# An FFT stage hidden in a matmul pipeline: folds and first-stage groups at other steps

## The chip, the cores and the metric

One core of a Trainium2 chip runs the whole program. The metric is the device time of one execution in microseconds; lower is better. The page of the profile names the engines PE (TensorE, matmuls), PEld (its weight loads), DVE (VectorE), ACT (ScalarE), POOL (GpSimd) and SP (SyncE, which here only issues DMAs).

## The reference

Two parts follow each other. The first is the real part of a two-dimensional FFT over sequence and model dimension of each of 8 batches; the second is a feed-forward block with a quick GELU on all 8 x 3008 tokens.

```python
X = np.fft.fft(x, axis=1)          # x: (8, 3008, 256) float32
X = np.fft.fft(X, axis=2)
x = X.real.astype(np.float32).reshape(8 * 3008, 256)
h = x @ w_in                       # (256, 2048)
g = h * (1.0 / (1.0 + np.exp(-1.702 * h)))
return (g @ w_out).astype(np.float32)   # w_out: (2048, 256)
```

## The kernel before

The FFT over the sequence is done in two stages of small matrix products (3008 = 47 x 64); the FFT over the model dimension is folded into `w_in`. The feed-forward block takes the result as its input. It is one long pipeline of **steps**: `steps` lists (batch, block, half, p) for 8 batches, 3 blocks, 2 halves and p = 0 to 7, so 384 steps `t`, 48 per batch. `t0 = 48 b` is the first step of batch b, and p = t mod 8. A run of 8 steps with one block and one half is one output tile of up to 256 tokens (226 in the second half of block 0, where `width(t)` is smaller); the 8 steps go over the hidden dimension in pairs.

In a step t (from step 8 on) the loop at the end of the kernel issues: `begin(t, 1)`, matmuls into a PSUM bank x (`halves`, L184); `forward(t)`, a GELU by ACT (L597); `product(t - 3)`, the second product of an earlier step (L184, tile o); `small_products` (L678, tile low), products of a fast matrix multiplication whose operands DVE makes; `begin(t + 1)`; `backward(t)` on DVE (L604), which reads the PSUM bank x; `doubled` (L600) and `activate_back` (L607) on ACT; `sums(t, gpsimd)` on POOL (L615, L616), which waits for L607; `sums(t - 1, vector)` on DVE in even steps (L622, L623), which needs the POOL sums; `deeper` on DVE (L644), which makes operands of `small_products`. Once every 8 steps an output tile is finished: ACT copies it (L747, L749, issued at p = 2), DVE adds (L750, L751, L779, worked at p = 3 and 4, then L761 and L797), ACT swaps halves at p = 4 (L787 to L789), DVE transposes (L730, issued at p = 5 and 6), and SP stores.

Beside this pipeline lies the FFT of the **next** batch, hung on steps by `at(t, fn, ...)`; what hangs on a step is issued at its end, in the order of the `at` calls, and each engine works its queue in order.

- `load_x(b + 2, k)`, four pieces, at t0 + 31, 33, 35, 37 (5 later for b = 0), SP: loads x into the only buffer `xt`, each after `paced`, a DMA of one element that waits for a result of that step and so holds SP's queue back.
- `fold1(b + 1, c, part)`, 16 **folds** per batch (c = 0 to 7, part 0 and 1), POOL, in place in `xt`. Part 0 is L225 and L227, part 1 is L230 and L231; the first one also makes the tile e (L218 to L220).
- `mix1(b + 1, m)`, four first-stage **groups** per batch, PE (L255) into two PSUM banks, then ACT copies back into `xt` (`mixed`, L263): one copy at once, the other in the next step behind `forward`. Group m needs folds 4m to 4m + 3 (counted as 2c + part). Its banks are the one that step t's x had, so it waits for `backward(t)`, and b2. Group 0 has 22 matmul instructions (8 of them on e), the others 16.
- `spill(b + 1, half, m)`, two DMAs per group, SP, one step after the group; later `fill` reads the result back.
- `stage2(b, blk)` at t0 + 8, 24 and 40 for the next block: PE matmuls L365 and DVE transposes L372.

A step with `mix1` or `stage2` is `special`, the one behind it is `after`: the ACT copies of `middle` (L585) for the step two ahead are then made one step later, and more of `product` is put ahead of `begin(t + 1)`.

Before the change the folds of a batch b >= 1 lay one a step at t0 + 6 to t0 + 21, and the groups at t0 + 12, 15, 19 and 23 (p = 4, 7, 3, 7). In batch 0 they lay at 11 to 26, and at 16, 20, 25 and 28. Batch 7 has none, since no batch follows.

Of the kernel before, what the change touches and what calls it, by code (L numbers as in the profile page):

```python
# [112 lines left out]
def kernel(ctx: ExitStack, tc, x, w_in, w_out, tab1, tab2, out):  # L113
    nc = tc.nc
# [807 lines left out]
    finish_out(0)  # L922

    extra, early = {}, {}

    def at(t, fn, *args):
        extra.setdefault(t, []).append((fn, args))
# [23 lines left out]
    for b in range(B):  # L951
        t0 = b * NBLK * NF
        late = 0 if b else 5
        if b + 2 < B:
            for k in range(3):
                at(t0 + 11 + k, paced, t0 + 11 + k)
                at(t0 + 11 + k, turn, b + 2, k)
        if b + 1 < B:
            for c in range(NCH):
                for part in range(2):  # L960
                    at(t0 + 6 + 2 * c + part + late, fold1, b + 1, c, part, nc.gpsimd)
                if c % 2:
                    k = t0 + 9 + 2 * c + late + (c == (5 if late else 1))
                    at(k, mix1, b + 1, c // 2)
                    for half in range(2):
                        at(k + 1, spill, b + 1, half, c // 2)
            for blk in range(NBLK):
                at(t0 + 27 + blk + late, paced, t0 + 27 + blk + late)
                at(t0 + 27 + blk + late, fill, b + 1, 4 * blk, 4 * blk + 4)
            if b + 2 < B:  # L970
                for k in range(4):
                    at(t0 + 31 + 2 * k + late, paced, t0 + 31 + 2 * k + late)
                    at(t0 + 31 + 2 * k + late, load_x, b + 2, k)
            at(t0 + 36 + 3 * (late > 0), rotate, b + 1)
        for blk in range(NBLK):
            nxt = (b, blk + 1) if blk + 1 < NBLK else (b + 1, 0)
            if nxt[0] < B:
                at(t0 + blk * NF + 8, stage2, *nxt)
                at(t0 + blk * NF + 9, nyquist_out, *nxt)
                at(t0 + blk * NF + 10, nyquist, *nxt)  # L980
# [123 lines left out]
```

## Time and profile before

| What | Value |
|---|---|
| Runs before | 1854.57, 1856.98, 1858.54 us; median 1856.98 us |
| The profiled execution | 1857.67 us; its span 1855.9 us; granted clock 0.999 |
| PE, PEld, DVE, ACT, POOL busy | 1838.7, 1401.5, 1514.7, 1151.2, 971.2 us |
| Folds: mean of L225, L227, L230, L231 | 0.47, 1.50, 0.89, 1.06 us, 56 of each |
| POOL sums L615, L616 | 0.94 and 0.94 us on average, 376 of each |

Busy time within a step differs much between values of p. Eight steps of batch 2 in which no fold and no group lies, from the busy times in windows of the trace (the window of p = 4 also holds `rotate`):

| p | window, us | length | DVE busy | ACT busy | POOL busy |
|---|---|---|---|---|---|
| 0 | 647.99:652.76 | 4.77 | 2.99 | 2.96 | 2.38 |
| 1 | 652.76:657.09 | 4.33 | 2.27 | 2.15 | 1.15 |
| 2 | 657.09:661.86 | 4.77 | 2.99 | 2.96 | 2.38 |
| 3 | 661.86:666.19 | 4.33 | 3.34 | 2.27 | 0.90 |
| 4 | 666.19:671.05 | 4.86 | 4.79 | 4.53 | 1.87 |
| 5 | 671.05:675.41 | 4.36 | 4.26 | 2.15 | 1.93 |
| 6 | 675.41:680.18 | 4.77 | 4.63 | 3.71 | 2.64 |
| 7 | 680.18:684.51 | 4.33 | 4.04 | 2.41 | 2.13 |

How to read it: PE has work almost all the time, so the length of a step is the time from one step's first matmul to the next step's; the first matmul of step t is the L184 row with tile x that follows the products of step t - 1. A step without extras takes 4.77 us at even p and 4.33 us at odd p (less in the narrower tile). What a group costs is read from how much longer its step and the ones behind it are than the same steps of batch 7. A POOL operation hung on step t is worked at the beginning of step t + 1, since POOL's sums of step t come first and wait for the end of step t.

### The profile page before, as it was taken

To read this page: it belongs to the slowest core of one execution; us is meant where nothing else is said; L and a number is where in the kernel's file an instruction comes from. 1 tells how busy PE (TensorE), PEld (TensorE's weight loads), DVE (VectorE), ACT (ScalarE), POOL (GpSimd) and SP (SyncE) were. 2 spreads that over 40 slices of the span, in tenths; PEclk is the share of its full clock that TensorE was granted. 3 is DMA by queue.
4 is the path that set the end of the run, shared out by engine and by line. 5 is a ranking of instruction groups with operands and counts; after the bars stand their busy time and mean duration, and the time that the engine had idled before them with its cause. 6 is when DMAs were issued, how large, how long until landed. Compare 5 with 4: busy or idle time off the path is not lost.

```text
span 1855.9 us, 56072 instructions
## 1 busy us (share of the span) xinstructions
PE 1838.7 (99%) x23722; PEld 1401.5 (76%) x23722; DVE 1514.7 (82%) x2112; ACT 1151.2 (62%) x2241; POOL 971.2 (52%) x1053
## 2 busy tenths in 40 slices
PE   8999999999999999999999999999999999999998
PEld 4677777777777777777777777777777777778776
DVE  6988778888788877987789878888888888878874
ACT  5756666666666656666566666666666666656663
POOL 4776446744367434773348633476445754434442
PEclk9999999999999999999999999999999999999999
DMA  8821340215012340223302132121411111100111
GB/s 265 196 61 34 84 68 19 72 49 102 19 38 53 73 84 13 51 50 88 59 13 64 45 86 53 18 75 35 103 30 24 36 46 36 30 19 13 23 20 24
DMA packets 149706, 105.31 MB, mean 57 GB/s; under 512 B 106057, under 2 KB 130665, under 8 KB 148896
## 3 DMA queue, kind: packets, MB, share of 16 engines
q1 hardware_dynamic: 146624, 99.68, 23.7%
q8 instruction: 187, 3.06, 0.7%
q10 hardware_dynamic: 2832, 2.05, 0.5%
q14 instruction: 63, 0.52, 0.1%
HBM read 64.41 MB, written 48.05 MB: 61 GB/s over the span
## 4 chain that ended last, share of the span: by engine, by line
PE 90%; DVE 5%; ACT 3%; DMA 1%; issue 1%; DVEq 0%; ACTq 0%
PE x L184 33%; PE o L184 26%; PE low L678 23%; PE o L678 4%; PE ps L255 2%; DVE big L644 2%; PE ps L365 1%; DVE big L779 1%; PE psw L184 1%; DMA xt<-in_x_dram 1%; DVE big L604 1%; ACT x L585 1%; DVE big L622 0%; DMA small<-in_tab_dram 0%; ACT g L597 0%
## 5 line engine op out<-in xcount | busy, mean ns | idle before, releaser
L615 POOL TENSOR_TENSOR big<-big 128x256 f32<-128x256 f32 (+1 forms) x376 | 352.0, 936 | 828.7 <-ACT big L607 676.9
L184 PE MATMUL x<-pq,wcs 128*64 128x256 f32 (+1 forms) x6016 | 769.0, 376 | 1.9 <-ACT g L597 1.6
L644 DVE TENSOR_TENSOR big<-big 128x512 f32<-128x512 f32 (+1 forms) x736 | 618.9, 855 | 23.1 <-PE low L678 4.7
L184 PE MATMUL o<-big,wo 128*64 128x256 f32 (+1 forms) x4800 | 620.8, 375 | 0.1
L184 PEld LDWEIGHTS x<-pq,wcs 128*64 128x64 f32 x6016 | 412.2, 137 | 186.1 <-issue 15.0
L184 PEld LDWEIGHTS o<-big,wo 128*64 128x64 f32 x4800 | 341.8, 137 | 147.8 <-DVE big L622 0.5
L597 ACT ACTIVATE g<-x 128x512 f32<-128x512 f32 (+1 forms) x376 | 221.7, 590 | 369.9 <-PE x L184 368.6
L604 DVE TENSOR_TENSOR big<-g,x 128x512 f32<-128x512 f32 (+1 forms) x376 | 249.9, 665 | 212.8 <-ACT big L600 212.6
L585 ACT ACTIVATE x<-nb,af 128x256 f32<-128x256 f32 (+1 forms) x752 | 352.9, 469 | 76.2 <-DVE pq L372 63.1
L678 PE MATMUL low<-big 128*64 128x128 f32 (+1 forms) x5888 | 382.9, 270 | 0.0
L678 PEld LDWEIGHTS low<-big 128*64 128x64 f32 x5888 | 337.6, 137 | 29.2
L616 POOL TENSOR_TENSOR big<-big 128x256 f32<-128x256 f32 (+1 forms) x376 | 351.5, 935 | 0.0
L600 ACT ACTIVATE big<-x 128x512 f32<-128x512 f32 (+1 forms) x376 | 219.2, 583 | 128.2 <-PE x L184 122.5
L607 ACT ACTIVATE big<-big 128x512 f32<-128x512 f32 (+1 forms) x376 | 231.9, 617 | 46.6 <-DVE big L604 44.4
L678 PE MATMUL low<-big,wo 128*64 128x128 f32 (+1 forms) x2944 | 220.5, 271 | 0.2
L678 PEld LDWEIGHTS low<-big,wo 128*64 128x64 f32 x2944 | 171.3, 137 | 4.5 <-DVE big L644 1.6
L623 DVE TENSOR_TENSOR big<-big 128x512 f32<-128x512 f32 (+1 forms) x188 | 166.6, 886 | 6.5
L622 DVE TENSOR_TENSOR big<-big 128x512 f32<-128x512 f32 (+1 forms) x188 | 137.1, 729 | 6.1 <-POOL big L615 6.1
L779 DVE TENSOR_TENSOR big<-big,low 128x512 f32<-128x512 f32 (+3 forms) x184 | 109.0, 609 | 3.5
L678 PEld LDWEIGHTS o<-big,wo 128*64 128x64 f32 x1472 | 92.3, 137 | 24.9
L678 PE MATMUL o<-big,wo 128*64 128x128 f32 (+1 forms) x1472 | 110.1, 270 | 0.0
L227 POOL TENSOR_TENSOR xt<-xt 111x510 f32<-111x510 f32 x56 | 83.7, 1495 | 4.4
(95 smaller groups left out, 964.5 us busy)
## 6 DMA issues: line engine op xcount, KB each, us to landing
out_dram<-os SPq DMA_DIRECT2D x284, 64.0 KB
t<-Td SPq DMA_DIRECT2D x22, 512.0 KB
Td<-xt SPq DMA_DIRECT2D x56, 192.0 KB
xt<-in_x_dram SPq DMA_DIRECT2D x14, 512.0 KB
xt<-Xr SPq DMA_DIRECT2D x14, 512.0 KB
nb<-Nd SPq DMA_DIRECT2D x23, 256.0 KB
out_dram<-os SPq DMA_DIRECT2D x96, 56.0 KB
Xr<-in_x_dram SPq DMA_DIRECT2D x7, 752.0 KB
```

What stands on the lines that cost most here:

```text
L184: nc.tensor.matmul(out[c0:c0 + 64], lhsT=lhs[:, c0:c0 + 64], rhs=rhs, skip_group_check=True, **how)
L585: nc.scalar.activation(x[:, i * 256:i * 256 + n], nbt[b, blk][:, hh * 256:hh * 256 + n], ACTF.Copy, scale=af1[:, f:f + 1])
L597: nc.scalar.activation(two(g[:], n), two(xb[t][:], n), ACTF.Copy, scale=2.0)
L600: nc.scalar.activation(front(t), two(xb[t][:], width(t)), ACTF.Gelu_apprx_sigmoid)
L604: nc.vector.tensor_tensor(back(t), two(gt.pop(t)[:], n), two(xb.pop(t)[:], n), op=ALU.subtract)
L607: nc.scalar.activation(back(t), back(t), ACTF.Gelu_apprx_sigmoid)
L615: eng.tensor_tensor(right(t, S1, n), left(t, A21, n), right(t, A22, n), op=ALU.add)
L616: eng.tensor_tensor(left(t, S3, n), left(t, A11, n), left(t, A21, n), op=ALU.subtract)
L622: eng.tensor_tensor(s2, s1, a11, op=ALU.subtract)
L623: eng.tensor_tensor(s4, a12, s2, op=ALU.subtract)
L644: nc.vector.tensor_tensor(out, i0, i1, op=how)
L678: nc.tensor.matmul(o, lhsT=lhs, rhs=rhs, start=first_in, stop=(p == NP - 2), skip_group_check=True)
```

## The change

From batch 1 on, folds and groups no longer follow a formula but a table. The list of folds and the list of groups give steps relative to t0, the third row for all batches from b = 2 on, so that negative numbers lie in the batch before. The table's first row repeats what batch 0 had. The spills stay one step behind their groups. `load_x`, `fill`, `rotate` and `stage2` stay where they are.

```diff
+    PLANS = ((range(11, 27), (16, 20, 25, 28)), ((-1, 0, 1, 1, 2, 7, 7, 9, 10, 15, 15, 16, 16, 17, 17, 18), (7, 15, 19, 23)),
+             ((-9, -7, -7, -6, -1, 0, 1, 1, 2, 7, 9, 10, 15, 16, 17, 17), (-1, 7, 15, 23)))
...
         if b + 1 < B:
+            folds, groups = PLANS[min(b, 2)]
             for c in range(NCH):
                 for part in range(2):
-                    at(t0 + 6 + 2 * c + part + late, fold1, b + 1, c, part, nc.gpsimd)
+                    at(t0 + folds[2 * c + part], fold1, b + 1, c, part, nc.gpsimd)
                 if c % 2:
-                    k = t0 + 9 + 2 * c + late + (c == (5 if late else 1))
+                    k = t0 + groups[c // 2]
                     at(k, mix1, b + 1, c // 2)
                     for half in range(2):
                         at(k + 1, spill, b + 1, half, c // 2)
```

In values of p: groups go from 4, 7, 3, 7 to 7, 7, 3, 7 in batch 1 and to 7, 7, 7, 7 in batches 2 to 6. Folds go from every p to p = 7, 0, 1 and 2, with two folds hung on one step in some places (in batch 1 at t0 + 1, 7, 15, 16 and 17; from batch 2 on at t0 - 7, 1 and 17), and none at the steps with `stage2`.

## The prediction, made before the changed kernel ran

> **What bounds the kernel.** I read the page first, busy times and the chain that ended last:
>
> ```profile
> PE 1838.7 (99%) x23722; PEld 1401.5 (76%) x23722; DVE 1514.7 (82%) x2112; ACT 1151.2 (62%) x2241; POOL 971.2 (52%) x1053
> ...
> PE 90%; DVE 5%; ACT 3%; DMA 1%; issue 1%; DVEq 0%; ACTq 0%
> ```
>
> PE is the bound, and its matmuls stay. So the change can only win the time in which PE is held up, and that is on the chain as DVE and ACT. How much there is: busy times in two windows, 16 steps from t0 + 8 on, in batch 2 (four groups, 16 folds) and in batch 7 (none). Columns: window, its length, then busy time (and count) of PE, PEld, DVE, ACT, POOL, clock, DMA.
>
> ```profile
> 533.93:610.20 76.27, 75.68 (x1032) 58.37 (x1029) 67.71 (x88) 47.47 (x96) 59.07 (x67) 1.00 0.22 55
> 1658.43:1728.69 70.26, 70.22 (x963) 55.99 (x961) 57.26 (x87) 44.47 (x90) 29.36 (x34) 1.00 0.10 20
> ```
>
> The FFT of the next batch costs 6.01 us here. DVE's busy time is 10.45 us higher with one instruction more: its instructions are held while POOL folds.
>
> **What a group costs at each place.** PE's timeline of batch 2 (start, length, engine, line, what, count). First t0 + 12 (p = 4, group 0), then t0 + 15 (p = 7, group 1), then t0 + 20, the step behind group 2 at t0 + 19 (p = 3):
>
> ```profile
> 552.62 0.93 PE L184 MATMUL x<-pq,wcs 128*64 128x226 f32 x8
> ...
> 556.07 0.94 PE L678 MATMUL low<-big 128*64 128x113 f32 x16
> 557.37 0.32 PE L255 MATMUL ps<-e,w 47*64 47x129 f32 x1 [0.35 <-DVE big L604]
> ...
> 558.83 0.98 PE L184 MATMUL x<-pq,wcs 128*64 128x226 f32 x8
> ```
> ```profile
> 570.64 0.55 PE L184 MATMUL o<-big,wo 128*64 128x226 f32 x4
> 571.12 1.09 PE L255 MATMUL ps<-xt,w 47*64 47x256 f32 x16
> 572.15 1.08 PE L184 MATMUL x<-pq,wcs 128*64 128x256 f32 x8
> ```
> ```profile
> 590.37 1.08 PE L184 MATMUL x<-pq,wcs 128*64 128x256 f32 x8
> ...
> 594.32 1.04 PE L678 MATMUL low<-big 128*64 128x128 f32 x16
> 595.59 1.08 PE L184 MATMUL x<-pq,wcs 128*64 128x256 f32 x8 [0.23 <-ACT g L597]
> ```
>
> At **p = 7** nothing waits. Group 1 takes 572.15 - 571.12 = 1.03 us, 0.10 more is lost going into it (570.64 to 571.12 is 0.48 for rows that take 0.38 elsewhere) and 0.05 in the first row behind it: 1.18 us, and the same at t0 + 23.
>
> At **p = 4** step t0 + 12 lasts 558.83 - 552.62 = 6.21 us; in batch 7 it lasts 1681.19 - 1676.97 = 4.22 us. So 1.99 us, and 0.15 in the next step (3.99 us against 3.83), 0.05 in the one after: 2.19. The chain of waits from 549.5 to 557.3 is DVE alone (L644, L750, L751, L604, four L779, three L644, L604): group 0 waits for L604 to leave the bank, and L604 stands behind the tile's additions, which fall on p = 3 and 4, in a step where DVE has 4.79 of 4.86 us to do anyway. At p = 7 it needs its own 558.83 - 557.37 = 1.46, plus 0.10 and 0.05: 1.61. **Gain 0.58 us per batch, batches 1 to 6.**
>
> At **p = 3** the group itself costs 1.12, but behind it step t0 + 20 loses 0.45 (5.22 us; 4.77 in batch 7), 0.05 of it the usual row. The chain there is ACT from 590.5 to 595.6: L263, two L585, L600, L263, L787 to L789, L597; the two copies of the group stand in the step of the swaps. At p = 7 the next step has p = 0, where ACT has 2.96 us to do; its two copies (0.58 each) fit in 4.77. **Gain 0.40 us per batch, batches 2 to 6; batch 1 keeps its group at t0 + 19.**
>
> Sum of the groups: 6 x 0.58 + 5 x 0.40 = **5.5 us**. A group now at t0 + 7 has `stage2` in the next step, as the one at t0 + 23 always had, which lost 0.05 us there; so I add nothing.
>
> **The folds.** Their number and POOL's work stay: a fold is 1.96 us (0.47 + 1.50, or 0.89 + 1.06), POOL's two sums 1.87. What changes is whom they hold. In batch 2 at p = 2 of t0 + 10, first DVE, then POOL:
>
> ```profile
> 546.16 1.09 DVE L622 TENSOR_TENSOR big<-big 128x452 f32<-128x452 f32 x1
> 547.28 2.29 DVE L623 TENSOR_TENSOR big<-big 128x452 f32<-128x452 f32 x1
> 549.49 0.68 DVE L644 TENSOR_TENSOR big<-big 128x512 f32<-128x512 f32 x1
> ```
> ```profile
> 546.73 1.11 POOL L231 TENSOR_TENSOR xt<-xt 111x254 f32<-111x254 f32 x1
> 547.80 0.66 POOL L615 TENSOR_TENSOR big<-big 128x226 f32<-128x226 f32 x1
> 548.42 0.66 POOL L616 TENSOR_TENSOR big<-big 128x226 f32<-128x226 f32 x1
> ```
>
> L623 takes 0.69 us in a step without folds (509.83) and 2.29 here: three POOL instructions pass it. The L644 behind it makes an operand that PE needs at p = 3; it ends at 550.17, and step t0 + 11 is 0.15 us longer than unhindered (4.13 us against 3.98). In step t0 + 2, without folds, the same L644 ends at 511.12 and PE uses it at 513.24. So **2.1 us of cover** lie between DVE at p = 2 and PE at p = 3, and one instruction passed over uses them up.
>
> The Trainium skill, page "SBUF — State Buffer", section "Who interferes with whom", says that a VectorE instruction with two SBUF inputs and a GpSimd one that reads SBUF shut each other out, and the second waits until the first has finished. By that alone an instruction would wait for one POOL instruction, the cover would hold and the sum would be the groups' 5.5 us; the 2.29 us row shows a wait through three, so the sum is made with the row.
>
> Folds taken from p = 3 to 6 free DVE where it is fullest. Worth at PE: between 0 and 0.10 us a batch (the odd 0.10 of step t0 + 13), and up to 1.1 us in all for hold-ups that only single batches show (step t0 + 12 is 2.25 instead of 1.99 over in batch 4, t0 + 14 0.56 instead of 0.05 in batch 5, t0 + 25 0.28 over in batch 3, each from the starts of the steps). I take 0.55.
>
> Two folds on one step are new. Hung on p = 1 they are worked at the start of p = 2, 3.9 us in a row, under L622, L623 and L644. No row shows that, so from both sides: 0.00 (step t0 + 19, p = 3 behind single folds at p = 1 and 2: 1.12 us over, just the group) and 0.37 us (step 19 of batch 0, 4.55 us against 4.18, also behind a group). I take the mean of 0.00 and the 0.15 above, 0.07, as the cover is the same; 3 places in each of 6 batches (batch 1 has five, of which three lie at p = 0 and 1) make 18 x 0.07 = **1.3 us lost**; ends 0 and 6.6. The fold hung on t0 + 10 stays, and its 0.15 with it.
>
> POOL's sums behind two folds come late: in batch 1, at t0 + 41, they ended at 472.2 and the next began at 474.4; 3.9 us of folds push that to 476.1. L622 needs them only in the next even step, which begins at 479.4 (p = 4), so nothing follows.
>
> **The early folds and SP.** The first fold, hung on t0 - 9, needs all of x. SP issues the last piece, `load_x` at t0 - 11, only at 456.06 and 457.10 (step 39.1 of batch 1); POOL is free for the fold at 461.5, 4.4 us later. If x lands late, POOL stands, and the first fold (4.4 us with e) pushes the sums from 463.95; L622 wants them at 472.8. So 463.95 + 1.9 may move by 7 us at no cost: price 0; 2 us a batch if the load takes over 10 us. The spills (two issues of 0.3 to 0.4 us per group) leave the place behind `paced` and `turn` (group 0's was issued at 568.5, step 15.3, though hung on 13). At t0 + 8 they stand ahead of the stores of `nyquist_out` and the load of nb, which is first read at step 16: 0.8 us of delay in 27 us of cover.
>
> **Sum:** -5.5 - 0.55 + 1.3 = -4.7 us. The profiled execution took 1857.67 us (span 1855.9 and 1.8 around it), 0.7 above the median of the runs. On the median, 1856.98: **1852.3 us**, 0.25% faster. About 0.2% (3.7 us) is what a measurement of this kernel can tell from no change.
>
> **Rivals.**
>
> 1. *The folds take back what the groups give* (0.14). Each of the 18 doubled places costs 0.37 us, the batch 0 row: 6.6 lost, -5.5 - 0.55 + 6.6 = +0.6: **1857.5**. For it: a single fold with sums behind it already used the whole cover. Against it: most L623 are not passed over by three.
> 2. *Slower: POOL in a row starves DVE at p = 2* (0.12). Two folds with sums before and behind are up to eight POOL instructions in a row. If two of L622, L623, L644 are passed over (1.6 us each) and the third waits 0.4, that is 3.6 us against 2.1 of cover: 1.5 at each of 18 places, 27 us, about **1878**; at half of them 1865. It decides from 0.33 us a place on ((5.5 + 0.55) / 18). Against it: fold instructions that follow each other (L230 and L231 in step t0 + 12) let a DVE instruction in between: 1.04 to 1.15 us each, 0.4 over.
> 3. *x lands late* (0.04): 5 batches x 2 us, -4.7 + 10 = **1862**. For it: 4.4 us is short. Against it: POOL has slack of 7 us.
>
> That the change does not do what it says is no rival worth a chance: steps are named outright; only batch 1's third group stays at p = 3.
>
> **How the numbers follow.** Forecast 0.70, own range 1849.5 to 1855.5 (the doubled places at 0 and at twice my figure, the single hold-ups at 0 and 1.1, and 1 us for the median); 0.07 of it lies above 1853.3, the bound of "faster". Faster 0.63; same 0.07 + 0.14 + half of rival 3 = 0.23; slower 0.12 + 0.02 = 0.14. The range for 8 in 10 goes from 1848.8 (no loss at doubled places, all single hold-ups gone) over rival 1 to 1860.
>
> **What would show it.** Right: steps with group 0 about 1.6 us over at p = 7, the step behind group 2 only 0.05 over, no DVE wait before L255. Wrong: PE waiting for L644 at p = 3 (t0 + 3, 19, 43) by more than 0.3 us; L623 of 3 us or more; POOL waiting for a DMA into xt; or a group at p = 7 over 1.3 us.

## The result, and the profile after

The changed kernel takes **1863.62 us** (median, 1862.84 to 1865.97), the kernel before 1855.71 us beside it (1854.57 to 1858.54): ratio 1.0044, 95% interval 1.0034 to 1.0054, so slower by 7.9 us. I had forecast 1852.3 us, 0.25% faster.

The page after the change, busy times and the chain by engine:

```profile
PE 1838.1 (99%) x23722; PEld 1398.8 (75%) x23722; DVE 1507.2 (81%) x2112; ACT 1151.5 (62%) x2241; POOL 945.2 (51%) x1053
...
PE 88%; DVE 6%; ACT 2%; issue 2%; DMA 1%; DVEq 0%; ACTq 0%
```

PE's share of the chain falls from 90 to 88%; DVE's rises, though DVE is busy 7.5 us less. The same 16 steps of batch 2, and below them batches 1 to 6 whole, in windows of the trace (length first, then busy time of PE, PEld, DVE, ACT, POOL); then batches 1 to 6 before:

```profile
534.15:608.89 74.74, 73.01 (x996) 56.75 (x992) 61.49 (x86) 46.65 (x94) 38.79 (x48) 1.00 0.20 50
269.84:1627.27 1357.43, 1346.03 (x17726) 1037.39 (x17724) 1111.15 (x1555) 847.23 (x1669) 699.81 (x793) 1.00 0.23 50
```
```profile
273.00:1622.12 1349.12, 1344.95 (x17726) 1038.91 (x17724) 1121.25 (x1555) 846.59 (x1669) 725.26 (x793) 1.00 0.23 50
```

The 16 steps are shorter (74.74 us against 76.27, with two groups instead of four), but batches 1 to 6 take 8.3 us more. That is the whole difference of the medians. The spans differ by only 5.2 us because these two executions came to step 8 at different times (its first matmul starts at 83.75 and 80.54 us), which has nothing to do with the change; so below I compare lengths of batches 1 to 6.

PE's timeline of the changed kernel shows where. Group 0 at its new place, then steps t0 + 3 and t0 + 19 of batch 2, which have no group:

```profile
493.67 0.60 PE L184 MATMUL o<-big,wo 128*64 128x256 f32 x4
494.20 0.32 PE L255 MATMUL ps<-e,w 47*64 47x129 f32 x1
...
495.64 1.08 PE L184 MATMUL x<-pq,wcs 128*64 128x256 f32 x8
```
```profile
510.43 1.04 PE L678 MATMUL low<-big 128*64 128x128 f32 x16
512.14 0.66 PE L678 MATMUL low<-big,wo 128*64 128x128 f32 x8 [0.67 <-DVE big L644]
...
584.46 0.94 PE L678 MATMUL low<-big 128*64 128x113 f32 x16
586.62 0.61 PE L678 MATMUL low<-big,wo 128*64 128x113 f32 x8 [1.21 <-DVE big L644]
```

Group 0 waits for nothing any more. But PE waits for L644 at p = 3, by 0.67 and 1.21 us of empty time. Over the whole run the waits of PE and PEld for L644 were small before (1.6 us for PEld, at most 0.2 for PE). Now (last columns: us in total, times, longest):

```profile
PEld low L678 <- DVE big L644: 12.6, 12, 1.4
PE low L678 <- DVE big L644: 9.8, 11, 1.2
```

PE waiting for L644 at p = 3 by more than 0.3 us was one of the signs of being wrong that I had named. Why L644 is late stands in DVE's and POOL's timelines at t0 + 2 and 3 of batch 2, behind the two folds hung on t0 + 1:

```profile
506.57 0.69 DVE L604 TENSOR_TENSOR big<-g,x 128x512 f32<-128x512 f32 x1 [0.77 <-ACT big L600]
507.17 1.27 DVE L622 TENSOR_TENSOR big<-big 128x512 f32<-128x512 f32 x1
508.48 2.47 DVE L623 TENSOR_TENSOR big<-big 128x512 f32<-128x512 f32 x1
510.87 1.21 DVE L644 TENSOR_TENSOR big<-big 128x512 f32<-128x512 f32 x1
```
```profile
506.63 1.26 POOL L227 TENSOR_TENSOR xt<-xt 111x510 f32<-111x510 f32 x1
507.97 1.06 POOL L230 TENSOR_TENSOR xt<-xt 111x254 f32<-111x254 f32 x1
508.99 0.72 POOL L231 TENSOR_TENSOR xt<-xt 111x254 f32<-111x254 f32 x1
509.67 0.73 POOL L615 TENSOR_TENSOR big<-big 128x256 f32<-128x256 f32 x1
510.36 1.18 POOL L616 TENSOR_TENSOR big<-big 128x256 f32<-128x256 f32 x1
```

L623 begins under L230 and ends while L616 stands; L231 and L615 run at their full speed (0.72 and 0.73 us) in between. The three DVE instructions take 0.58 + 1.78 + 0.52 = 2.88 us longer than the 0.69 us of each without folds. The cover was 2.12 us (511.12 to 513.24 in the kernel before) less the 0.06 from L644's end to PE's start, so 2.06 us, and 0.82 us are left over; the step is 0.89 us longer.

The same pair of folds (part 0 and part 1 of one c) hangs on t0 + 1 of batch 1, and there t0 + 3 loses nothing. POOL comes 0.7 us later there (L227 begins 2.5 us after the step, in batch 2 1.8 us), so L622 is through before the folds:

```profile
281.31 0.68 DVE L622 TENSOR_TENSOR big<-big 128x512 f32<-128x512 f32 x1
282.03 1.65 DVE L623 TENSOR_TENSOR big<-big 128x512 f32<-128x512 f32 x1
283.60 1.21 DVE L644 TENSOR_TENSOR big<-big 128x512 f32<-128x512 f32 x1
```
```profile
281.48 1.65 POOL L227 TENSOR_TENSOR xt<-xt 111x510 f32<-111x510 f32 x1
```

The three are 1.47 us over, and that fits into the cover. So a doubled place (a step on which two folds hang) does not always have this price; what differs in these rows is the moment at which POOL begins the pair.

Each step's length less the shortest that the same place of a batch takes in any batch (from the starts of PE's first x matmul; at t0 + 11, where batch 0 is shorter than all others, less that of batch 7), summed over batches 1 to 6, in us:

| place | before | after | e1_single | e5_group0_p4 |
|---|---|---|---|---|
| t0 + 12, 13 (before and e5: group 0) | 13.2 | 0.3 | 0.3 | 8.5 |
| t0 + 7 (not before: group 0 hung in batch 1, else group 1) | 0 | 7.2 | 7.2 | 7.2 |
| t0 + 47 and 0 (after and e1: group 0) | 0 | 8.0 | 8.0 | 0 |
| t0 + 3 | 0 | **4.5** | 0 | 0 |
| t0 + 15 and 23 (a group each, in all four) | 13.5 | 13.5 | 13.5 | 13.5 |
| t0 + 19 (group 2: before in all batches, else in batch 1) | 6.7 | **8.4** | 1.2 | 1.2 |
| t0 + 20 | 2.7 | 0.5 | 0.5 | 0.5 |
| t0 + 6 | 0 | 0.8 | 0.1 | 0.1 |
| t0 + 14 | 0.8 | **2.5** | 2.6 | 0.5 |
| t0 + 11 | 1.1 | 0 | 0 | 0 |
| all 48 places | 48.4 | 56.7 | 44.6 | 42.8 |

The rows leave out 10.3 to 11.4 us at other places, most of it at t0 + 40 with its `stage2` (7.1 us in all four).

### The profile page after: what moved, and what is told of

Its sections match the earlier page's. It is cut to its first block, busy times and chain, and to the rows that moved or that the text cites. A ratio compares the mean times of both kernels' runs of the same rounds, so it can differ in the third digit from the quotient of the medians.

```text
span 1861.1 us, 56058 instructions
## 1 busy us (share of the span) xinstructions
PE 1838.1 (99%) x23722; PEld 1398.8 (75%) x23722; DVE 1507.2 (81%) x2112; ACT 1151.5 (62%) x2241; POOL 945.2 (51%) x1053
## 4 chain that ended last, share of the span: by engine, by line
PE 88%; DVE 6%; ACT 2%; issue 2%; DMA 1%; DVEq 0%; ACTq 0%
PE x L184 32%; PE o L184 25%; PE low L678 23%; PE o L678 4%; DVE big L644 2%; PE ps L255 2%; DVE big L622 1%; PE ps L365 1%; DVE big L604 1%; DMA xt<-in_x_dram 1%; PE psw L184 1%; DVE big L779 1%; ACT big L600 1%; ACT x L585 0%; DMA small<-in_tab_dram 0%
## 5 line engine op out<-in xcount | busy, mean ns | idle before, releaser
L615 POOL TENSOR_TENSOR big<-big 128x256 f32<-128x256 f32 (+1 forms) x376 | 346.7, 922 | 861.6 <-ACT big L607 777.6
L644 DVE TENSOR_TENSOR big<-big 128x512 f32<-128x512 f32 (+1 forms) x736 | 611.9, 845 | 24.1 <-PE low L678 3.9
L604 DVE TENSOR_TENSOR big<-g,x 128x512 f32<-128x512 f32 (+1 forms) x376 | 249.9, 665 | 237.0 <-ACT big L600 236.9
L585 ACT ACTIVATE x<-nb,af 128x256 f32<-128x256 f32 (+1 forms) x752 | 352.6, 469 | 69.6 <-DVE pq L372 56.4
L616 POOL TENSOR_TENSOR big<-big 128x256 f32<-128x256 f32 (+1 forms) x376 | 359.8, 957 | 0.0
L607 ACT ACTIVATE big<-big 128x512 f32<-128x512 f32 (+1 forms) x376 | 232.0, 617 | 55.3 <-DVE big L604 52.5
L623 DVE TENSOR_TENSOR big<-big 128x512 f32<-128x512 f32 (+1 forms) x188 | 156.0, 830 | 6.5
L622 DVE TENSOR_TENSOR big<-big 128x512 f32<-128x512 f32 (+1 forms) x188 | 144.2, 767 | 2.7 <-POOL big L615 2.7
L227 POOL TENSOR_TENSOR xt<-xt 111x510 f32<-111x510 f32 x56 | 77.0, 1375 | 4.4
```

What stands on the lines that cost most here:

```text
L585: nc.scalar.activation(x[:, i * 256:i * 256 + n], nbt[b, blk][:, hh * 256:hh * 256 + n], ACTF.Copy, scale=af1[:, f:f + 1])
L604: nc.vector.tensor_tensor(back(t), two(gt.pop(t)[:], n), two(xb.pop(t)[:], n), op=ALU.subtract)
L607: nc.scalar.activation(back(t), back(t), ACTF.Gelu_apprx_sigmoid)
L615: eng.tensor_tensor(right(t, S1, n), left(t, A21, n), right(t, A22, n), op=ALU.add)
L616: eng.tensor_tensor(left(t, S3, n), left(t, A11, n), left(t, A21, n), op=ALU.subtract)
L622: eng.tensor_tensor(s2, s1, a11, op=ALU.subtract)
```

## The experiments

All start from the changed kernel and edit the third row of its table (batches 2 to 6); e8, e9 and e10 also edit `fold1`. Theories: **A**, two folds hung on one step hold DVE past its cover; **B**, packing all folds into p = 7 to 2 does; **C**, the groups' places do.

**e1_single: no step with two folds.**

```diff
-             ((-9, -7, -7, -6, -1, 0, 1, 1, 2, 7, 9, 10, 15, 16, 17, 17), (-1, 7, 15, 23)))
+             ((-9, -8, -7, -6, -1, 0, 1, 2, 7, 8, 9, 10, 15, 16, 17, 18), (-1, 7, 15, 23)))
```


> Third row of the table: no step has two folds (-9, -8, -7, -6, -1, 0, 1, 2, 7, 8, 9, 10, 15, 16, 17, 18); groups as in the changed kernel. Theory A (two folds hung on one step at p = 1 hold L622, L623 and L644 of p = 2, and PE waits at p = 3): steps t0 + 3 and t0 + 19 of batches 2 to 6 lose 0 to 0.2 us instead of 0.89 and 1.43, about 10.5 us in all, time 1853 us. Theory B (what costs is that all folds are packed into p = 7 to 2, doubled or not): both steps keep at least half of their loss, time 1858 us or more. Theory C (the groups at p = 7 are what costs): no change, 1863 us.

Measured: 1851.75 us, ratio to before 0.9982 (0.9972 to 0.9991). The losses at t0 + 3 and t0 + 19 are gone. DVE at t0 + 18 of batch 3:

```profile
807.96 1.45 DVE L622 TENSOR_TENSOR big<-big 128x512 f32<-128x512 f32 x1
809.44 0.69 DVE L623 TENSOR_TENSOR big<-big 128x512 f32<-128x512 f32 x1
810.05 1.16 DVE L644 TENSOR_TENSOR big<-big 128x452 f32<-128x452 f32 x1
```

L623 has its free 0.69 us again; L622 still waits for L227. A holds for batches 2 to 6, B and C fall: with the same groups, and folds in the same values of p, the kernel is faster than before.

**e2_each_step: one fold a step, p = 3 to 6 too.** Third row: `(range(-9, 7), (-1, 7, 15, 23))`.

> Third row: one fold on each step from t0 - 9 to t0 + 6, so p = 3 to 6 too; groups as in the changed kernel. Theory A: no doubled folds, so the losses at t0 + 3 and t0 + 19 go; those at p = 3 to 6 that a single fold causes are 0.1 to 0.4 us a batch, time 1853 to 1855.5 us. If folds at p = 3 to 6 are what the change rightly avoided, they cost over 0.6 us a batch, and this kernel is over 3 us slower than the one with single folds at p = 7 to 2. Theory C: 1863 us.

Measured: 1868.87 us, ratio 1.0073 (1.0058 to 1.0088), the slowest of all. So my figure for single folds at p = 3 to 6 was far off. PE at t0 + 6 and 7 of batch 2, and DVE before and there:

```profile
529.22 1.08 PE L184 MATMUL x<-pq,wcs 128*64 128x256 f32 x8 [0.60 <-ACT x L585]
...
534.05 0.65 PE L184 MATMUL o<-big,wo 128*64 128x256 f32 x4 [0.28 <-DVE big L622]
```
```profile
521.46 1.18 DVE L622 TENSOR_TENSOR big<-big 128x512 f32<-128x512 f32 x1
...
525.73 1.29 DVE L797 TENSOR_TENSOR big<-big 128x768 f32<-128x768 f32 x1
526.95 0.68 DVE L604 TENSOR_TENSOR big<-g,x 128x512 f32<-128x512 f32 x1
...
530.51 0.64 DVE L604 TENSOR_TENSOR big<-g,x 128x512 f32<-128x512 f32 x1
531.08 2.92 DVE L622 TENSOR_TENSOR big<-big 128x512 f32<-128x512 f32 x1
```

Two holds stand here. On the way from p = 4 to 5 single folds hold L622 and L797, which take 0.69 and 0.96 us at the same place of e1_single. So L604 comes 0.8 us late, behind it ACT's L607 and L585, and PE waits 0.60 us for L585: t0 + 6 loses 0.82 us. At p = 6 one fold and the sums behind it (L227 to 532.08, L615, L616) pass L622, and the group at t0 + 7 costs 1.99 instead of 1.12 us in batches 2 to 6. In batches 1 to 5, t0 + 46 loses 0.82 to 1.41 us, and the group at t0 + 47 costs 0.8 more. With the groups at p = 7, folds are rightly kept off these steps. The kernel before had folds there at a small loss; probably the longer step t0 + 12 of its group 0 gave DVE the time, but no run tests that.

**e3_old_groups: the new folds, the old groups.** Third row's groups: `(12, 15, 19, 23)`.

> Third row: folds as in the changed kernel, groups where they were before (t0 + 12, 15, 19, 23). Theory A: t0 + 3 keeps its 0.89 us, t0 + 19 its 1.43 beside the group; groups cost 0.98 us a batch more than in the changed kernel, and the loss at t0 + 14 (0.2 to 0.6) is gone, since DVE catches up while PE waits at t0 + 12: 1865 to 1867 us. Theory C: the time falls to about that of the kernel before, 1856 us.

Measured: 1863.78 us, ratio 1.0046 (1.0031 to 1.0061), as the changed kernel. t0 + 3 and t0 + 19 keep their losses (0.98 and 1.44 beside the group), so the folds alone make the kernel slower and C falls again. I expected 1 to 3 us more. Group 0 at p = 4 shows why not:

```profile
550.60 0.93 PE L184 MATMUL x<-pq,wcs 128*64 128x226 f32 x8
...
554.92 0.32 PE L255 MATMUL ps<-e,w 47*64 47x129 f32 x1
...
556.36 0.98 PE L184 MATMUL x<-pq,wcs 128*64 128x226 f32 x8
```

No wait for L604 now, and the step is 5.76 us long, 1.55 over, not 1.99: with no fold at p = 3 and 4, p = 4 costs 1.55 + 0.16 + 0.05 = 1.76 us against 1.60 at p = 7. And the loss at t0 + 14 of batches 2 to 6 is gone.

**e4_order: doubled places with the pair the other way round**, part 1 of one c and part 0 of the next.

```diff
-             ((-9, -7, -7, -6, -1, 0, 1, 1, 2, 7, 9, 10, 15, 16, 17, 17), (-1, 7, 15, 23)))
+             ((-9, -7, -7, -6, 0, 1, 1, 2, 7, 8, 9, 10, 16, 17, 17, 18), (-1, 7, 15, 23)))
```


> Third row: folds -9, -7, -7, -6, 0, 1, 1, 2, 7, 8, 9, 10, 16, 17, 17, 18, groups as in the changed kernel: as many doubled places at p = 1 as in the changed kernel, but each pair is now part 1 of one c and part 0 of the next (L230, L231, L225, L227), as at t0 - 7, where nothing was lost. If the order in the pair decides (L227, L230 and L231 in a row and then the sums pass L623): t0 + 3 and t0 + 19 lose 0 to 0.2 us, 1853 to 1854 us. If it is the number of folds in a row: they keep 0.9 and 1.4 us, 1863 us.

Measured: 1852.87 us, ratio 0.9984 (0.9975 to 0.9994). t0 + 19 loses nothing, t0 + 3 0.24 us. So it is not simply the number of folds in a row. DVE at t0 + 2 of batch 2:

```profile
507.09 1.17 DVE L622 TENSOR_TENSOR big<-big 128x512 f32<-128x512 f32 x1
508.30 0.69 DVE L623 TENSOR_TENSOR big<-big 128x512 f32<-128x512 f32 x1
508.90 2.45 DVE L644 TENSOR_TENSOR big<-big 128x512 f32<-128x512 f32 x1
```

With this order L623 gets through in 0.69 us, and the long hold falls on L644. The three together are 2.24 us over 0.69 each, not 2.88. Their sum gives the loss at t0 + 3 in five cases: 2.88 us over, 0.89 lost (changed kernel); 2.98 over, 0.98 lost (e3); 2.24 over, 0.24 lost (here); 1.47 over (batch 1) and 1.12 over (e1_single), nothing lost. In these cases the cover is 2.0 us in effect, and what exceeds it is lost in full.

**e6_one_double: e1_single with one doubled place**, 17, 17 in place of 17, 18.

> e1_single with one edit: the fold hung on t0 + 18 goes to t0 + 17, so one doubled place at p = 1 (part 0 and part 1 of one c). If the doubled place is the whole cause: t0 + 19 loses 1.4 us in each of batches 2 to 6 and nothing else changes, 7 us in all, 1858 to 1860 us. If it takes both doubled places to make POOL late: t0 + 19 loses under 0.5 us, 1853 us.

Measured: 1857.96 us (one run). t0 + 19 loses 1.44 us in each of batches 2 to 6; batches 1 to 6 are 7.4 us longer than in e1_single. So this doubled place has its whole price without the other one.

**e7_double_p0: the doubled place on p = 0**, 16, 16 in place of 15, 16.

> e1_single with one edit: folds 15, 16 become 16, 16, so one doubled place hung on p = 0 (part 0 and part 1 of one c), worked at the start of p = 1. If the harm needs L622 and L623 of an even step underneath, because L644 behind them has only 2 us of cover: no step near t0 + 18 loses over 0.2 us, 1851 to 1853 us. If any two folds in a row hold DVE past its cover: t0 + 18 or t0 + 19 loses about 1 us in each batch, 1856 to 1858 us.

Measured: 1858.04 us, ratio 1.0015 (1.0006 to 1.0024); t0 + 19 loses 1.45 us. My first reading falls: it need not be L622 and L623 that are passed. DVE of batch 3 from t0 + 17 on:

```profile
803.15 4.90 DVE L644 TENSOR_TENSOR big<-big 128x452 f32<-128x452 f32 x3
807.98 0.67 DVE L604 TENSOR_TENSOR big<-g,x 128x512 f32<-128x512 f32 x1
808.57 1.45 DVE L622 TENSOR_TENSOR big<-big 128x512 f32<-128x512 f32 x1
```

Three L644 take 4.90 us (2.84 in e1_single), L604 follows without the 0.59 us that DVE stood idle there, and the delay is handed on to the L644 that PE needs at p = 3. The cover is one for p = 1 and 2 together.

**e5_group0_p4: e1_single with group 0 back at p = 4.**

```diff
-             ..., (-1, 7, 15, 23)))
+             ..., (12, 7, 15, 23)))
```


> Third row: the single folds of the kernel e1_single, groups (12, 7, 15, 23): group 0 goes back to p = 4, the others stay at p = 7. If the wait at p = 4 is DVE's own excess of work at p = 3 to 6 that PE has to wait for somewhere, then with no folds at p = 4 the group there costs 1.75 us (1.55 + 0.16 + 0.05) against 1.60 at p = 7, and the loss at t0 + 14 (0.2 to 0.6 us a batch) goes: 0.1 to 0.4 us a batch won, 1850 to 1851.5 us. If p = 4 is dear by itself, as my prediction had it (0.58 us more), the time is 1854 to 1855 us and t0 + 14 keeps its loss.

Measured: **1849.55 us, ratio 0.9972 (0.9963 to 0.9981)**, faster than both kernels; batches 1 to 6 take 1343.5 us, 1.8 less than in e1_single. The loss at t0 + 14 is gone in batches 2 to 6, group 0 costs 1.76 us. PE at t0 + 12 and DVE at t0 + 13 of batch 2:

```profile
554.55 0.32 PE L255 MATMUL ps<-e,w 47*64 47x129 f32 x1
...
556.00 0.98 PE L184 MATMUL x<-pq,wcs 128*64 128x226 f32 x8
```
```profile
558.24 0.62 DVE L604 TENSOR_TENSOR big<-g,x 128x452 f32<-128x452 f32 x1
```

PE does not wait for group 0 here, as in e3. But the group makes step t0 + 12 1.55 us longer, and DVE catches up in this time: L604 begins 2.24 us after the start of its step, in the changed kernel 3.80 us (560.77, the step begins at 556.97). DVE is nearly full at p = 4 and 5 (4.79 of 4.86 us and 4.26 of 4.36 in the table before the change). In these runs PE either works a group at p = 4 in the meantime or waits for DVE's excess at p = 6.

**e8_no_folds: e1_single without its folds for batches 3 to 7.**

> e1_single without the fold instructions L225, L227, L230 and L231 for batches 3 to 7; the tile e, the groups and the rest stay, so the output is not the reference's. Shows what single folds at p = 7 to 2 still cost. If they cost nothing there and the loss at t0 + 14 is DVE's own: t0 + 14 keeps about 0.26 us as in batch 7, groups cost 1.60 and 1.18 us, and the time is 1 to 2 us under e1_single, 1850 us. If folds still cost: more than 3 us under e1_single.

Measured: 1853.05 us (one run, step 8 begun at 85.2 us against 82.7 in e1_single); batches 1 to 6 are 2.3 us shorter than in e1_single. Of that 1.2 us are won at t0 + 14, which loses 0.08 to 0.27 us here in batches 2 to 6 (0.26 in batch 7) against up to 0.61, and 0.9 at t0 + 43 of batch 2, where single folds hold L623 for 3.02 us in e1_single. The time as a whole is above the 1850 us I expected, since this execution came late to step 8. Single folds at p = 7 to 2 are nearly free, with that one exception.

**e9_pause and e10_best_pause: a short POOL instruction behind each fold.**

```diff
         eng.tensor_tensor(free(t, up + H + 1, [-D, 2], [1, H - 1]), fwd, rev, op=ALU.subtract)
+        eng.memset(rest_[:], 0.0)
```


> e6_one_double (one doubled place, hung on t0 + 17) with one small POOL instruction more, a memset of 128x4 that nothing reads, behind every part 1 of a fold. If a held DVE instruction is passed because POOL's next instruction follows the one before without a gap, the short one lets L623 in before the sums: L623 takes about 1.2 us less, t0 + 19 loses about 0.3 us instead of 1.44, 1852 to 1853.5 us. If the work of the two folds itself is what DVE waits for, the memset changes nothing or adds to it: t0 + 19 loses 1.4 us or more, 1858 us.

> e5_group0_p4 with the same memset behind every part 1 of a fold. There no doubled place is left, so there is little to win: if the pause helps, the losses left in batch 0 and at t0 + 43 of batch 2 shrink, 1848 to 1849.5 us; if it only adds POOL work, 1849.5 to 1850.5 us.

Measured: 1858.72 us, ratio 1.0021 (1.0011 to 1.0030), and 1849.42 us, ratio 0.9970 (0.9957 to 0.9982). With one doubled place t0 + 19 still loses 1.48 us. DVE, and then POOL at the same place (L232 is L231 of the other kernels, L617 is L615, L625 is L623):

```profile
809.48 2.52 DVE L625 TENSOR_TENSOR big<-big 128x512 f32<-128x512 f32 x1
```
```profile
809.99 0.72 POOL L232 TENSOR_TENSOR xt<-xt 111x254 f32<-111x254 f32 x1
810.65 0.09 POOL L233 MEMSET rest__97<- 128x4 f32 x1
810.71 0.73 POOL L617 TENSOR_TENSOR big<-big 128x256 f32<-128x256 f32 x1
```

The memset of 0.09 us lets nobody in, and the idea behind it falls. What decides whether a waiting DVE instruction gets in after one POOL instruction (1.1 to 1.7 us) or only after three (2.3 to 3.0) stays open; batch 1 and e4 show only that it changes with the moment and the order.

## Why the prediction was wrong

**The step that failed** is the price of a doubled place: "I take the mean of 0.00 and the 0.15 above, 0.07, as the cover is the same; 3 places in each of 6 batches (...) make 18 x 0.07 = 1.3 us lost". It measured 0.89 us at t0 + 3 and 1.44 at t0 + 19 in each of batches 2 to 6, 11.7 us, another 0.8 us at t0 + 6 (there in the changed kernel, e3 and e4, but 0.1 in e1_single and e6), nothing at t0 - 7 in most batches (0.5 us once), and in batch 1 nothing at t0 + 3 and 0.11 us at t0 + 19 beside the group. My two rows had a single fold above the cover; with two folds and the sums behind, three DVE instructions in a row are held, and 2.9 us do not fit where 2.1 do. At t0 + 19 it is worse: L622 is held longer (1.44 us), and the step before takes PE 4.42 us instead of 4.77, since it still works products of the narrower tile. The mean of two rows told how far single folds come, not what the sum of holds under two would be. The slower rival came near: 1.5 us a place, 1865 us (1864.4 by its terms) if half of the places have it. Ten of 18 places lost 1.2 us on average, and 1863.6 us came out. That is in part luck, since the rival had two instructions passed over at 1.6 us each; the rows show one (1.78 us over) and two shorter holds.

**Group 2 from p = 3 to 7**: right. Step t0 + 20 is 4.77 us long, the 0.40 us a batch are won, 2.0 in all.

**Group 0 from p = 4 to 7**: right in its size at the new place (1.60 us, forecast 1.61) and won there (3.9 us with the wait, forecast 3.5), wrong in its cause, so that the agreement is in part luck. I put the wait down to the place; e3 and e5 show that 0.43 of the 0.58 us are gone without the folds at p = 3 and 4, and that the longer step t0 + 12 let DVE catch up. Without it, the loss at t0 + 14 grows from 0.8 to 2.5 us. There PE waits in the changed kernel for the ACT copies L585, behind L607, behind L604, behind DVE's additions (L797), here in batch 2:

```profile
559.89 0.96 DVE L797 TENSOR_TENSOR big<-big 128x768 f32<-128x768 f32 x1
560.77 0.62 DVE L604 TENSOR_TENSOR big<-g,x 128x452 f32<-128x452 f32 x1
```
```profile
561.42 0.59 ACT L607 ACTIVATE big<-big 128x452 f32<-128x452 f32 x1 [1.34 <-DVE big L604]
```
```profile
562.88 0.79 PE L184 MATMUL x<-pq,wcs 128*64 128x226 f32 x6 [0.39 <-ACT x L585]
```

I had no term for this, and in batch 7 before, without any fold or group, step t0 + 14 was already 0.26 us too long.

**Folds off p = 3 to 6**: I gave it at most 0.10 us a batch and 1.1 in all. e2 shows over 3 us a batch when nothing else holds PE before p = 6. The stall I expected to stay, 0.15 us at t0 + 11, went (1.1 us in all).

**x landing late, late sums, the spills**: right at no cost. The waits after list none of POOL for a DMA into xt, and DVE's L622 waits for POOL's L615 2.7 us in all, 6.1 before.

**The rule of the Trainium skill** ("SBUF — State Buffer", "Who interferes with whom"), that the second of two such instructions waits until the first has finished, gives 1.27 us for L622 but not the 2.47 us of L623, which waits through L230, L231 and L615. By the rule, at one hold of about 0.6 us for each of the three (an estimate from L622 and L644), 1.7 us would have fitted into the cover. The measurement decides.

## What to carry to other kernels

Work moved to an idle engine still has a price if that engine shares something with the busy one: measure how long the busy engine's instructions are held under it, add up all that lie on one chain up to the next use, and compare the sum with the cover. Spread such work singly where you can: here two pieces in a row cost 0.9 to 1.45 us at ten of 18 places, and single ones nearly nothing. Two pieces at another moment (batch 1) or in another order (e4) cost at most 0.24 us, so look at each place and not at the count alone. And before taking work or a wait of the bound engine out of a step, ask which late engine used that time to catch up: its excess comes back at the next place, here from p = 4 to p = 6.

## What the hardware showed that I had not expected

A DVE instruction with both inputs in SBUF can wait through three POOL instructions in a row: 2.47 us for L623 at every 1, 1 and 17, 17 of batches 2 to 6 and up to 3.02 us (t0 + 42 of batch 2 in e1_single, behind single folds), against 0.69 us free. It repeats within 0.01 us from batch to batch; when POOL comes 0.7 us later (batch 1) it is 1.65 us, and with another order of the same folds (e4) it moves to another instruction. So it is not chance; that the moment decides is likely, but not shown. The way to step 8 varies by up to 4.9 us between the profiled executions of these kernels, which do the same work up to there (80.4 to 85.2 us), while batches 3 to 6 of e5_group0_p4 repeat within 0.03 us (223.57 to 223.60); small differences are better read from a stretch of steps than from a span.
